# Two transformer layer types: the ratio of the exponential sums put ahead of the key sums, and the reciprocal denominator put behind the numerators

## The chip, the cores and the metric

One core of a Trainium2 chip. Its engines run side by side, each through its own list of instructions in order: TensorE (PE, with PEld for its weight loads), VectorE (DVE), ScalarE (ACT), GpSimd (POOL) and SyncE (SP, which here issues the transfers). They wait for each other by semaphores. The metric is the device time of one execution in microseconds (us); the median of three runs of the kernel before is 319.74 us (319.6 to 320.0).

## The reference

`x` is 2048 tokens of 512 numbers, bf16. Four residual layers are run in the order A, B, A, B, with the same weights in both passes; each adds to `x` an attention of the layernormed `x`. There are 32 heads of 16 numbers.

```
# layer A, linear attention, per head
pq, pk = q @ w_phi, k @ w_phi
phi_q = [softmax(pq), softmax(-pq)]          # 32 features
phi_k = [softmax(pk), softmax(-pk)]
kv, z = phi_k.T @ v, phi_k.sum(tokens)       # the "key sums"
o = (phi_q @ kv) / (phi_q . z + 1e-6)
# layer B: softmax attention of each token over 8 tokens at distances 0, 2, ..., 14
# both: x = x + o @ wo
```

Layer A's two softmaxes of a query have the denominators S0 = sum exp(pq) and S1 = sum exp(-pq). With E0 = exp(pq) and E1 = exp(-pq), o = (E0.kv0/S0 + E1.kv1/S1) / (E0.z0/S0 + E1.z1/S1), and the same value comes out when both parts of the fraction are multiplied by S0, as (E0.kv0 + (S0/S1) E1.kv1) / (E0.z0 + (S0/S1) E1.z1).

## The kernel before

The tokens are worked on in 4 blocks of 512 (4 tiles `t` of 128 tokens). `wqkv` and `w_phi` are folded into one matrix WA at the start. A layer A then has these steps for each block `b`; names are those of the code, lines those of the profile.

- Keys (`s_a1`): projections of keys (L632) and values (L644), exp of plus and minus the key features on ACT (Ek, L638), their sums over 16 features by four halving additions on DVE (L665 to L678), the reciprocals as Ln and Exp on ACT (L684, L685), Ek times these on DVE (L690), and the key sums on PE (`kv`, L707): per tile 16 matmuls with the values as weights (33 columns: 32 values and a one) and Ek as the moving side (2 x 32 columns), two side by side in the array. All blocks add into one PSUM bank, which a matmul with zeros opens (L700).
- Queries (`s_a2`): projections (L737, 4 x 4 matmuls of 512 columns), exp of both signs on ACT (Eq, L745), sums over features on PE (`ms`, L753, 32 matmuls), Ln and Exp of both sums on ACT (L759, L760: rS = 1/S0 and 1/S1).
- Between (`s_akv`), once per layer, after the last key sum: the bank is copied to SBUF (kvT, L202 or L204), turned by four transposes (L783), and masked into ZM (L792, for denominators) and R (L796, for numerators).
- Denominators (`s_a3`): `md` (L821, 32 matmuls of Eq with ZM), then on DVE D times rS and the sum of both (L829, L832), on ACT Ln and Exp (L835, L836), on DVE rho = rS/denominator for both signs (L840). Rho is spread to all 128 rows: in blocks 0 and 1 by PE (`bc`, L847, 16 matmuls per sign) and multiplied into all 8 pieces of Eq on DVE (L855, straight from PSUM, or from a copy bs that ACT makes at L886); in blocks 2 and 3 by two transfers through DRAM (Prho) and two DVE products of 2048 columns (L875).
- Numerators (`s_a4`): `mo` (L940, 32 matmuls of the scaled Eq with R), four copies out of PSUM (oT, by ACT or DVE), the output projection (L553), residual addition (L571, or by a matmul with the identity, L556, and an ACT copy), layernorm sums, and transposes for layer B (L482), whose projections are L967.

Nothing is scheduled at run time. Every step is a closure in a thread of its stage and engine; the string `_ORDER` lists the threads in the order in which the next closure of each is recorded, so it fixes the order of each engine. `_CHOICE` says for each movable copy whether DVE (1) or ACT (0) makes it, and `_SLOTS` which buffer or PSUM bank each tile takes. All three came from a search outside the kernel. `_OPT` is the same before and after.

Of the kernel before, what the change touches and what calls it, by code (L numbers as in the profile page):

```python
# [8 lines left out]
BF16 = mybir.dt.bfloat16  # L9
# [24 lines left out]
VCH = NB * 8 * DV  # L34
EST = (1, 3)
# [25 lines left out]
8 2 i 2e 3s e3 ce 2p 23 i a 5l i i 9 i i i 5o i i i i 4e e7 1m i 0 3u 3r 0 f i e c j b 2 k 3 4 j o 5q 1m l 3 m  # L61
p 1n 0 i 1 n 1t e4 o 1o q 1m 1p r 0 1m 1u s 1m z 5k z z 5 1m 1r 7 6 z 20 20 7 1q 1s 1t 21 21 t 20 20 1v 22 10
z 22 1t 7 1t 20 1w 22 t 11 24 24 13 u 12 16 12 1t t 15 1t v 12 12 22 x 18 14 1x d w w 1y 2c y 18 18 26 18 2d
1f 2d 2c 1z 2d 24 2d 27 17 19 18 1a 1b 21 1c 1d 22 21 22 39 1e 20 20 22 39 25 2c 3b 3a 3a 1f 3a 2d 3a 2f 2c 1f
1f 39 ch 22 2f 2d 2g 1g 29 1f 2d 1j 2f 2d 7 1h 29 1i 1k 3a 29 2n 29 2i 2n 3c 2o 2o 2o 2k 2o 2k 2q 1l cd 2h 2n
2a 2k 2f 2n 2k 3a 2o 2j 24 2q 2r 2q 2o 2o 2o 29 2y 28 2y 2y 3c 2l 2z 2v 2z 2s 2z 2z 2k 2y 2z 39 36 31 2z 36 2z
3a 3b 36 36 2v 31 2v 37 2v 31 2t 36 2z 36 2b 2b 2b 2b 2m 2m ci 36 36 2m 3a 2w 2m 2v 33 34 32 31 3c 35 2q 3c 36
3b 2x g 2x 2u 2x 30 37 2x 36 38 38 38 38 3i 3c 3h 3c 39 3b 3a 3j 3k 3k 3k 3c 3d 3c 3e 3l 3b 3m 3d 3e 5h 3n 3m
3c 3e 3e 3l 5i 3m 3q 3m 3m 4f 3m 3d 3l 5j 3e 3e 3m 5i 3m 3m 3v 3d 3e 3e bd 5h 5m 5n 5i 5i 5i 3m 3d 3e 7c 5h 7d
5p 5i 5i 5i 5r 3f 3g 3g 5i 3f 3g 5i 3w 3f 3z 3x 3f 3g 5s 3y 7e 40 41 3g 7d 5u 5v 7f 5t 3g 3p 41 42 41 41 44 3g  # L70
43 3g 43 5w 5x 5x 7f 45 46 43 43 47 43 7f 5y 3f 90 47 48 49 3g 4c 91 5x 41 4b 41 41 41 4a 92 5x 4d 60 91 4l 5z
61 5z 93 5z 4q 62 5z 4g 7d 4g 4g 4m 4q 63 ck 5z 7d 4r 93 4i 4l 63 66 64 67 7g 4s 7j 65 7h 7i 4h 4j 7k bo 4n 4q
4q 4u 4w 91 7l 4t 7l 7l 7m 7l 7o 68 7n 7n 4l 7p 3h 7n 7q 4w 93 4v 7n 4v 3o 91 4f 6a 7r 4o 6b 7n 6k 6f 69 4g 4k
4l 7r 6l 7s h 4w 6g 6k 6m 4p 6a 6c 6p 7t 7u 6a 6k 6f 6n 7v 4w 6k 6h 94 6r 6d 4x 4x b2 6r 4x 97 6o 98 4x 95 6f
# [36 lines left out]

_SLOTS = {
    "med": (
        "b79ca642352f85de6b0464b12833892cb7516e70efd8561f1706ed4a53bc7430e3f9eba731f9cd011a4091d20483b8ae4c4f"
        "b71d6236f9ec40bfd6ea7830c4"
    ),
    "ps": (
# [2008 lines left out]
```

## Time and profile before

| what | value |
|---|---|
| median of 3 runs | 319.74 us (319.6 to 320.0) |
| span of the profiled execution | 318.1 us |
| what lies around the span, by the median | 1.6 us |
| PE busy | 307.7 us, 97% |
| DVE busy | 295.6 us, 93% |
| ACT busy | 275.0 us, 86% |
| granted PE clock | full in all 40 slices |

The profile gives one execution's span only; what lies around it is the difference to the median of the runs. "Busy" counts the stretches in which at least one instruction of the engine is under way. A matmul of 512 columns is shown with 380 ns, but the next one starts about 216 ns later, so that PE's busy time hides pauses shorter than about 160 ns. Times in the text are counted from the span's start. The layer A parts lie at about 11 to 76 us and 145 to 230 us, the layer B parts at 76 to 178 us and from 224 us to the end.

### The profile page before, as it was taken

The numbers are of one execution on the slowest core, as the hardware profiler recorded it, in microseconds if no ns is written. First come the engines' busy times: TensorE is split into PE (matmuls) and PEld (weight loads), VectorE is DVE, ScalarE is ACT, GpSimd is POOL, SyncE is SP. The second block draws the span as 40 slices with busy tenths as digits, with TensorE's granted clock in tenths as the row PEclk, the third lists the DMA queues.
The fourth block names the chain that finished last, engine by engine and source line by source line (L and its number), as shares of the span: only waits on it lengthen the run. The fifth ranks groups of instructions, "written<-read, shape, count | busy, mean of one in ns | idle before, by whom it ended". The sixth has DMA issues, their size and how long they took to land.

```text
span 318.1 us, 8900 instructions
## 1 busy us (share of the span) xinstructions
PE 307.7 (97%) x3578; PEld 152.9 (48%) x3578; DVE 295.6 (93%) x459; ACT 275.0 (86%) x639; POOL 47.2 (15%) x60
## 2 busy tenths in 40 slices
PE   8999999899999999999999999989999999999994
PEld 4644456445454444444444455544444544444552
DVE  6999996998999999999999999689998999999994
ACT  4999999999898778999999999899999867697751
POOL 6000000000004212000000000033141644045000
PEclk9999999999999999999999999999999999999999
DMA  7977100005794989939894600004289875565664
GB/s 203 358 186 148 36 2 4 2 19 145 165 178 100 156 141 136 144 66 140 145 134 62 69 0 2 4 19 134 59 185 137 140 133 134 105 178 126 158 152 170
DMA packets 45789, 36.37 MB, mean 114 GB/s; under 512 B 30832, under 2 KB 41136, under 8 KB 45744
## 3 DMA queue, kind: packets, MB, share of 16 engines
q1 hardware_dynamic: 45216, 35.75, 56.3%
q8 instruction: 29, 0.48, 0.7%
q14 instruction: 16, 0.13, 0.2%
q10 hardware_dynamic: 528, 0.02, 0.1%
HBM read 11.13 MB, written 3.25 MB: 45 GB/s over the span
## 4 chain that ended last, share of the span: by engine, by line
PE 87%; DVE 5%; ACT 5%; DMA 1%; issue 1%; SPq 0%; DVEq 0%; ACTq 0%
PE PS L967 23%; PE PS L553 18%; PE PS L632 9%; PE PS L644 9%; PE PS L737 6%; PE PS L1128 4%; PE PS L1066 4%; PE PS L1185 2%; DVE Eq L855 2%; PE PS L707 2%; PE PS L940 1%; PE PS L482 1%; PE PS L556 1%; PE PS L1200 1%; PE PS L1082 1%; DMA x<-in_A_x_dram 1%
## 5 line engine op out<-in xcount | busy, mean ns | idle before, releaser
L967 PE MATMUL PS<-xnT,WB 128*128 128x512 bf16 x336 | 76.8, 380 | 0.1
L1059 DVE TENSOR_TENSOR prod<-QT,K 128x4096 bf16<-128x4096 bf16 x28 | 63.4, 2287 | 0.5 <-POOL K L993 0.5
L1121 DVE TENSOR_TENSOR pav<-PT,Vg 128x4096 bf16<-128x4096 bf16 (+1 forms) x29 | 62.9, 2214 | 0.2
L967 PEld LDWEIGHTS <-WB 128*128 128x128 bf16 x336 | 37.3, 114 | 36.4 <-issue 3.3
L745 ACT ACTIVATE Eq<-PS 128x512 bf16<-128x512 f32 x64 | 36.3, 619 | 0.0
L638 ACT ACTIVATE Ek<-PS 128x512 bf16<-128x512 f32 x64 | 35.1, 622 | 0.2 <-PE PS L632 0.2
L553 PEld LDWEIGHTS <-oT 128*128 128x128 bf16 x236 | 21.9, 98 | 26.6 <-issue 1.3
L737 PE MATMUL PS<-xnT,WA 128*128 128x512 bf16 x128 | 32.0, 380 | 0.5 <-DVE s L829 0.3
L578 ACT ACTIVATE sqd<-x 128x512 bf16<-128x512 bf16 x48 | 29.9, 631 | 2.2 <-DVE x L571 2.0
L644 PE MATMUL PS<-WA,xnT 128*128 128x512 bf16 x128 | 31.6, 379 | 0.0
L632 PE MATMUL PS<-WA,xnT 128*128 128x512 bf16 x128 | 31.0, 379 | 0.2 <-ACT WA L204 0.2
L571 DVE SCALAR_TENSOR_TENSOR x<-PS,x 128x512 bf16<-128x512 f32 x46 | 30.2, 684 | 0.7 <-PE PS L553 0.7
L204 ACT CAST oT<-PS 128x512 bf16<-128x512 f32 (+1 forms) x50 | 26.7, 597 | 3.8 <-PE PS L1128 2.1
L553 PE MATMUL PS<-WoA,oT 128*128 128x512 bf16 x128 | 29.8, 380 | 0.0
L553 PE MATMUL PS<-WoB,oT 128*128 128x512 bf16 x108 | 26.5, 379 | 0.0
L204 ACT CAST K<-PS 128x512 bf16<-128x512 f32 x30 | 17.3, 593 | 3.1 <-PE PS L967 1.9
L632 PEld LDWEIGHTS <-xnT 128*128 128x128 bf16 x128 | 12.3, 98 | 15.2 <-issue 1.0
L644 PEld LDWEIGHTS <-xnT 128*128 128x128 bf16 x128 | 12.2, 98 | 14.5 <-issue 0.4
L690 DVE TENSOR_TENSOR Ek<-Ek,rk 128x4096 bf16<-128x4096 bf16 (+1 forms) x10 | 18.6, 1860 | 0.4 <-ACT rk L685 0.4
L737 PEld LDWEIGHTS <-WA 128*128 128x128 bf16 x128 | 11.6, 98 | 14.6 <-issue 1.7
L466 DVE TENSOR_SCALAR xn<-x,rstd,nmr 128x512 bf16<-128x512 bf16 x48 | 18.1, 424 | 0.6
L204 ACT CAST V<-PS 128x512 bf16<-128x512 f32 x26 | 15.2, 596 | 2.6 <-PE PS L967 2.6
(175 smaller groups left out, 505.1 us busy)
## 6 DMA issues: line engine op xcount, KB each, us to landing
Vg<-V SPq DMA_DIRECT2D x112, 131.5 KB, 4.3
Prho<-rd SPq DMA_DIRECT2D x8, 512.0 KB, 6.1
x<-in_A_x_dram SPq DMA_DIRECT2D x3, 512.0 KB, 6.6
WB<-in_B_wqkv_dram SPq DMA_DIRECT2D x3, 512.0 KB, 9.8
out_dram<-x SPq DMA_DIRECT2D x6, 256.0 KB, 2.3
wraw<-in_A_wqkv_dram SPq DMA_DIRECT2D x4, 256.0 KB, 4.5
vd<-Vs SPq DMA_DIRECT2D x2, 272.0 KB, 2.9
x<-in_A_x_dram SPq DMA_DIRECT2D x4, 128.0 KB, 3.4
```

Of the source, the lines that this page charges most:

```text
L204: self.nc.scalar.copy(out=out, in_=in_)
L553: nc.tensor.matmul(y[:], lhsT=lh(t, c), rhs=Wo()[:, c, :], start=(c == 0), stop=(c == NB - 1 and not onpe))
L571: nc.vector.scalar_tensor_tensor(out=xb[:, t, :], in0=T[t][:], scalar=1.0, in1=xb[:, t, :], op0=ALU.mult, op1=ALU.add, **kw)
L578: nc.scalar.activation(out=sqd[:], in_=xb[:, t, :], func=ACT.Square, accum_out=T["ss"][:, t:t + 1])
L632: nc.tensor.matmul(pk[:], lhsT=xnT[:, t, k, :], rhs=self.WA[:, k, D:2 * D], start=(k == 0), stop=(k == NB - 1))
L638: nc.scalar.activation(out=T["E"][:, t, s, :], in_=T["k", t][:], func=ACT.Exp, scale=1.0 - 2.0 * s)
L644: nc.tensor.matmul(pv[:], lhsT=xnT[:, t, k, :], rhs=self.WA[:, k, 2 * D:3 * D], start=(k == 0), stop=(k == NB - 1))
L737: nc.tensor.matmul(pq[:], lhsT=self.WA[:, k, hb * P:(hb + 1) * P], rhs=xnT[:, :, k, :], start=(k == 0), stop=(k == NB - 1))
L745: nc.scalar.activation(out=self.Eq[L, b][s][:, :, hb, :], in_=T[hb][:].rearrange("p (t i) -> p t i", t=4), func=ACT.Exp, scale=1.0 - 2.0 * s)
L967: nc.tensor.matmul(pp[:], lhsT=self.WB[:, k, i * D + c:(i + 1) * D:NB], rhs=xnT[:, :, k, :], start=(k == 0), stop=(k == NB - 1))
L1059: nc.vector.tensor_tensor(out=pr[:], in0=QT[:, c:c + 1, :].to_broadcast([P, NW, TB]), in1=win, op=ALU.mult)
L1121: nc.vector.tensor_tensor(out=pv, in0=PT[:, :, lo:lo + n].unsqueeze(1).to_broadcast([P, NB, 2, n]), in1=vw, op=ALU.mult)
```

## The change

Of each query's two sums only the ratio w = S0/S1 is formed (`ls`, `lw`, `w`: Ln of both sums on ACT, a subtraction on DVE, Exp on ACT). It is spread to all rows by PE in every block (`bc` in `s_a2`, L770 of the new kernel) and multiplied into the four pieces of E1 alone (`mulw`, L784, from PSUM or from ACT's copy bs). These steps need no key sums. `md` (L847 of the new kernel) then adds both signs in one PSUM range, ACT takes Ln and Exp of it (L855, L857), and this one reciprocal (rho) is spread: in blocks 0 and 1 by PE (L863) and four copies to an SBUF tile Prho (`rev`, ACT or DVE), in blocks 2 and 3 by one transfer through DRAM. `mo` (L919) works on Eq as it is, and rho comes in as the numerators leave PSUM: DVE multiplies each of the four PSUM banks with a slice of Prho (`ev` in `s_a4`, L929). Those 32 evictions were copies on ACT or DVE before.

The key sums change sides: the weights are 128 columns of Ek (64 of each sign) and the values move (65 columns), 8 matmuls per tile over the whole array, 256 in all instead of 512 (L704). They come out with features on the rows, so the transposes, kvT's copy and the opening matmul go; four copies of 64 x 260 (`sh`) bring them into R, half of 1e-6 is added to the features' own sums (`z`), and ZM is filled and R masked in place (`r`).

The three tables are new throughout. Choices that moved: DVE's copies of oT fall from 11 to 1 and ACT's from 48 to 26 (with 32 products instead), DVE's vaug copies rise from 7 to 11, six of 48 layernorm applications (xn) go from DVE to ACT, and 17 residuals on PE become 19.

On DVE in the first layer A, before, from the copy of the key sums (kvT) on; `s1`, `Ds` and `rho` belong to the denominators, `Eq` to the queries:

```order
L202 CAST kvT_121<-PS_88 128x512
L792 TENSOR_TENSOR ZM0_122<-PS_88,maskH_97 128x2x2x8 x2
L796 TENSOR_TENSOR R_126<-PS_88,mask2_98 128x256
L829 TENSOR_TENSOR s1_1086<-PS_88,rS_1004 128x256
L832 TENSOR_TENSOR Ds_1088<-s1_1086 128x128
L840 TENSOR_TENSOR rho_1130<-rS_1004,Ds_1088 128x256
L829 TENSOR_TENSOR s1_1153<-PS_88,rS_1132 128x256
L832 TENSOR_TENSOR Ds_1155<-s1_1153 128x128
L855 TENSOR_TENSOR Eq_467<-PS_88,Eq_467 128x512 x2
L855 TENSOR_TENSOR Eq_467<-bs_1158,Eq_467 128x512
L855 TENSOR_TENSOR Eq_467<-PS_88,Eq_467 128x512
L855 TENSOR_TENSOR Eq_469<-PS_88,Eq_469 128x512
```

Now the same place, from the last ratio ahead of the copy of the key sums (R) on:

```order
L760 TENSOR_TENSOR lw_953<-lS_873 128x128
L204 CAST R_125<-PS_88 64x4x65
L784 TENSOR_TENSOR Eq_462<-bs_891,Eq_462 128x512
L784 TENSOR_TENSOR Eq_462<-bs_875,Eq_462 128x512
L811 TENSOR_SCALAR R_125<-R_125 128x8
L819 TENSOR_TENSOR ZM0_121<-R_125,maskH_97 128x4x4x2 x2
L784 TENSOR_TENSOR Eq_513<-PS_88,Eq_513 128x512 x4
L760 TENSOR_TENSOR lw_1081<-lS_1072 128x128
L823 TENSOR_TENSOR R_125<-R_125,mask4_98 128x8x64
L784 TENSOR_TENSOR Eq_918<-PS_88,Eq_918 128x512 x2
L204 CAST Prho_1169<-PS_88 128x512 x3
L929 TENSOR_TENSOR oT_1228<-PS_88,Prho_1169 128x512 x4
```

The products with the whole rho (two signs, 16 pieces for two blocks) gave way to products of E1 with the ratio, which stand around the copy of the key sums; behind them now stand copies of rho (Prho) and the products that empty the numerators (oT), ahead of the first residuals.

In the second layer A of the changed kernel, DVE from the copies of the key sums on:

```order
L204 CAST R_125<-PS_88 64x4x65 x3
L784 TENSOR_TENSOR Eq_3002<-bs_3276,Eq_3002 128x512
L784 TENSOR_TENSOR Eq_3002<-PS_88,Eq_3002 128x512
L811 TENSOR_SCALAR R_125<-R_125 128x8
L819 TENSOR_TENSOR ZM1_122<-R_125,maskH_97 128x4x4x2 x2
L784 TENSOR_TENSOR Eq_3002<-bs_3283,Eq_3002 128x512
L784 TENSOR_TENSOR Eq_3002<-PS_88,Eq_3002 128x512
L823 TENSOR_TENSOR R_125<-R_125,mask4_98 128x8x64
L784 TENSOR_TENSOR Eq_2448<-bs_2826,Eq_2448 128x512
L204 CAST Prho_3409<-PS_88 128x512 x3
L760 TENSOR_TENSOR lw_3517<-lS_3482 128x128
L929 TENSOR_TENSOR oT_3540<-PS_88,Prho_3409 128x512 x4
```

And ACT there, from the first reciprocal denominator (rho) on; `lS` and `w` make the last block's ratio:

```order
L857 ACTIVATE rho_3383<-Ds_3381 128x128
L742 ACTIVATE Eq_3292<-PS_88 128x4x128
L855 ACTIVATE Ds_3402<-PS_88 128x128
L857 ACTIVATE rho_3404<-Ds_3402 128x128
L742 ACTIVATE Eq_3286<-PS_88 128x4x128
L742 ACTIVATE Eq_3292<-PS_88 128x4x128
L855 ACTIVATE Ds_3477<-PS_88 128x128
L857 ACTIVATE rho_3479<-Ds_3477 128x128
L756 ACTIVATE lS_3482<-PS_88 128x256
L206 CAST Prho_3409<-PS_88 128x512
L764 ACTIVATE w_3520<-lw_3517 128x128
```

Here DVE's row `lw` needs ACT's `lS`, which stands behind the last exps of Eq and three pairs of Ds and rho, and DVE's oT products are queued behind that `lw`. On PE the steps between the last key sum and the first output projection are now, in order: bc of a ratio, 12 query projections, `md` of two blocks, 4 projections, bc of a rho, `md` of one block, `ms` of the last block, `mo` of the first block, bc of the last ratio, bc of a rho. Before, they were: the transposes, `ms`, `md`, 4 projections, `md`, bc, 4 projections, bc, `md`, 8 projections, `mo`, `ms`, bc. In the first layer A they are now: 8 projections, bc of a ratio, `md`, 4 projections, `ms`, `md`, bc of a ratio, 4 projections, bc of a rho, 4 projections, `mo`, bc of a rho, 4 projections, `mo`, and the first output projection (4 matmuls and one with the identity), then `ms` of the last block.

```diff
--- before.py
+++ after.py
+HQ = 4 * DH
+KVC = HQ + 1
...
 _ORDER = """
-8 2 i 2e 3s e3 ce 2p 23 i a 5l i i 9 i i i 5o i i i i 4e e7 1m i 0 3u 3r 0 f i e c j b 2 k 3 4 j o 5q 1m l 3 m
-p 1n 0 i 1 n 1t e4 o 1o q 1m 1p r 0 1m 1u s 1m z 5k z z 5 1m 1r 7 6 z 20 20 7 1q 1s 1t 21 21 t 20 20 1v 22 10
...
+8 i i bu 2 i i 0 i 2 a 0 3 i 2e 4 3 i 1m 1 9 i 0 c e i 0 i f 1m 7 i b j 5 o k j l 1n 1o p 1t 1m m i o 1m q r 20
...
         def ek(t, s):
             if t == 0 and s == 0:
-                T["E"] = self.big([4, 2, D], "Ek")
-            nc.scalar.activation(out=T["E"][:, t, s, :], in_=T["k", t][:], func=ACT.Exp, scale=1.0 - 2.0 * s)
+                T["E"] = self.big([4, 8, 2, HQ], "Ek")
+            nc.scalar.activation(out=T["E"][:, t, :, s, :], in_=T["k", t][:].rearrange("p (g c) -> p g c", c=HQ),
+                                 func=ACT.Exp, scale=1.0 - 2.0 * s)
...
         def ev(t, dve):
             vatile()
-            self.copy(dve, T["va"][:, t, :, 0:H], T["v", t][:].rearrange("p (a c) -> p a c", c=H))
+            self.copy(dve, T["va"][:, t, :, 0:HQ], T["v", t][:].rearrange("p (g c) -> p g c", c=HQ))
...
         def kv(t):
             if L not in self.kvp:
-                self.kvp[L] = self.ps()
-            K = self.kvp[L]
-            if b == 0 and t == 0:
-                nc.tensor.matmul(K[:], lhsT=self.kvT[:, 0:P], rhs=self.kvT[:], start=True, stop=True)
-            for r in range(4):
...
-                        nc.tensor.matmul(out, lhsT=T["va"][:, t, q, :], rhs=T["E"][:, t, :, q * H:(q + 1) * H],
-                                         start=(b == 0 and t == 0 and r == 0 and h2 == 0),
-                                         stop=(b == 3 and t == 3), tile_position=(0, 64 * c), skip_group_check=True)
+                self.kvp[L] = [self.ps() for _ in range(2)]
+            for g in range(8):
+                c = g // 2 * KVC
+                nc.tensor.matmul(self.kvp[L][g % 2][:, c:c + KVC], lhsT=T["E"][:, t, g, :, :],
+                                 rhs=T["va"][:, t, g, 0:KVC], start=(b == 0 and t == 0 and g < 2),
+                                 stop=(b == 3 and t == 3), skip_group_check=True)
...
-        def rs():
-            r = self.sm([2, P], "rS", F32, 4)
-            nc.scalar.activation(out=r[:], in_=T["S"][:, 0:2 * P], func=ACT.Ln)
-            nc.scalar.activation(out=r[:], in_=r[:], func=ACT.Exp, scale=-1.0)
-            self.rS[L, b] = r
+        def ls():
+            T["l"] = self.sm([2, P], "lS", F32, 2)
+            nc.scalar.activation(out=T["l"][:], in_=T["S"][:, 0:2 * P], func=ACT.Ln)
+
+        def lw():
+            T["lw"] = self.sm([P], "lw", F32, 2)
+            nc.vector.tensor_tensor(out=T["lw"][:], in0=T["l"][:, 0, :], in1=T["l"][:, 1, :], op=ALU.subtract)
+
+        def w():
+            T["w"] = self.sm([P], "w", BF16, 2)
+            nc.scalar.activation(out=T["w"][:], in_=T["lw"][:], func=ACT.Exp)
+
+        def bc():
+            T["pb"] = [self.ps() for _ in range(4)]
+            for hb in range(NB):
+                for t in range(4):
...
+        def mulw(t, direct):
+            ev = self.Eq[L, b][1][:, t, :, :]
+            src = T["pb"][t] if direct else T["bs", t]
+            nc.vector.tensor_tensor(out=ev, in0=src[:].rearrange("p (a i) -> p a i", a=NB), in1=ev, op=ALU.mult)
...
         add(st, "PE", ms)
-        add(st, "ACT", rs)
+        st = "aw_%d%d" % (L, b)
+        add(st, "ACT", ls)
+        add(st, "DVE", lw)
+        add(st, "ACT", w)
+        add(st, "PE", bc)
+        for t in range(4):
+            direct = _CHOICE[self.nflex] == "1"
+            self.flex(st, bev, t)
+            add(st, "DVE", mulw, t, direct)
...
+        def sh(half, s, dve):
+            self.copy(dve, R[HQ * half:HQ * half + HQ, s, :, 0:KVC],
+                      self.kvp[L][half][HQ * s:HQ * s + HQ, 0:NB * KVC].rearrange("p (b c) -> p b c", c=KVC))
...
+        def z():
+            nc.vector.tensor_scalar(out=R[:, :, :, HQ:KVC], in0=R[:, :, :, HQ:KVC], scalar1=DEN_EPS / 2, scalar2=None,
+                                    op0=ALU.add)
...
+            v = R[:, :, :, 0:HQ].rearrange("p s b (j d) -> p (s b) j d", d=DH)
+            nc.vector.tensor_tensor(out=v, in0=v, op=ALU.mult,
+                                    in1=self.mask4[:].unsqueeze(1).unsqueeze(3).to_broadcast([P, 8, 4, DH]))
+
+        for half in range(2):
+            for s in range(2):
+                self.flex(st, sh, half, s)
+        add(st, "DVE", z)
+        add(st, "DVE", r)
...
     def s_a3(self, L, b, dma):
...
             for s in range(2):
                 for hb in range(NB):
                     for t in range(4):
-                        nc.tensor.matmul(Dp[32 * t:32 * t + 32, s * P:(s + 1) * P],
+                        nc.tensor.matmul(Dp[32 * t:32 * t + 32, 0:P],
                                          lhsT=zm[:, self.reg(s, hb) * H:(self.reg(s, hb) + 1) * H],
                                          rhs=self.Eq[L, b][s][:, t, hb, :], start=(hb == 0 and s == 0),
-                                         stop=(hb == NB - 1), tile_position=(0, 32 * t), skip_group_check=True)
...
+                                         stop=(hb == NB - 1 and s == 1), tile_position=(0, 32 * t),
+                                         skip_group_check=True)
+
+        def ln():
             T["Ds"] = self.sm([P], "Ds", F32, 1)
-            nc.vector.tensor_tensor(out=T["Ds"][:], in0=T["DR"][:, 0, :], in1=T["DR"][:, 1, :], op=ALU.add)
-
-        def ln():
+            nc.scalar.activation(out=T["Ds"][:], in_=T["D"][:, 0:P], func=ACT.Ln)
+            T["rho"] = self.sm([P], "rho", BF16)
+            nc.scalar.activation(out=T["rho"][:], in_=T["Ds"][:], func=ACT.Exp, scale=-1.0)
...
+            for r in range(4):
                 for t in range(4):
+                    nc.tensor.matmul(T["pb"][t][:, r * P:(r + 1) * P], lhsT=self.indB[32 * t:32 * t + 32, r, :, :],
+                                     rhs=T["rho"][32 * t:32 * t + 32, :], start=True, stop=True,
                                      tile_position=(32 * t, 0))
...
+        def ptile():
+            pr = self.med([4, 4, P], "Prho")
+            for r in range(4):
+                self.rho[L, b][r] = pr[:, :, r, :]
+            return pr
+
+        def rev(t, dve):
+            if "pr" not in T:
+                T["pr"] = ptile()
+            self.copy(dve, T["pr"][:, t, :, :].rearrange("p r i -> p (r i)"), T["pb"][t][:])
...
+            pr = ptile()
...
+            src = bass.AP(a.tensor, a.offset, [[pitch, 16], [0, 8], [1, 16 * P]])
+            nc.sync.dma_start(out=pr[:].rearrange("p t r i -> p (t r i)"), in_=src)
+
+        self.rho[L, b] = {}
         add(st, "PE", md)
...
         add(st, "ACT", ln)
-        add(st, "DVE", rho)
         if dma:
             add(st, "SP", wr)
-            for s in range(2):
-                add(st, "SP", rdb, s)
-            for s in range(2):
-                add(st, "DVE", muld, s)
+            add(st, "SP", rdb)
             return
...
+        add(st, "PE", bc)
+        for t in range(4):
+            self.flex(st, rev, t)
...
-                                         lhsT=self.R[32 * r:32 * r + 32, self.reg(s, hb), :],
+                                         lhsT=self.R[32 * r:32 * r + 32, s, hb, 32 * (r % 2):32 * (r % 2) + 32],
...
-        def ev(r, k, m, dve):
+        def ev(r, k, m):
...
-            self.copy(dve, self.oT[key, b][:, r, k * w:(k + 1) * w], T[r][:, k * w:(k + 1) * w])
+            n = 4 // m
+            nc.vector.tensor_tensor(
+                out=self.oT[key, b][:, r, k * w:(k + 1) * w].rearrange("p (t i) -> p t i", t=n),
+                in0=T[r][:, k * w:(k + 1) * w].rearrange("p (t i) -> p t i", t=n),
+                in1=self.rho[L, b][r][:, k * n:(k + 1) * n, :], op=ALU.mult)
...
             for r in range(4):
-                self.flex(st, ev, r, k, m)
+                add(st, "DVE", ev, r, k, m)
```

248 lines of the change are left out of this document (89 added, 159 removed).

## The prediction

> **What bounds the kernel now.** I read the page first: what is busy, and on what the chain of waits stands.
>
> ```profile
> span 318.1 us, 8900 instructions
> PE 307.7 (97%) x3578; PEld 152.9 (48%) x3578; DVE 295.6 (93%) x459; ACT 275.0 (86%) x639; POOL 47.2 (15%) x60
> PE 87%; DVE 5%; ACT 5%; DMA 1%; issue 1%; SPq 0%; DVEq 0%; ACTq 0%
> ```
>
> PE bounds it, with DVE close behind; 10% of the chain stands on DVE and ACT. Where that is, the busy time by stretches tells: a quiet part of layer B, and the two places around and behind the last key sum of each layer A.
>
> ```profile
> core 0: us, PE busy (x) PEld busy (x) DVE busy (x) ACT busy (x) POOL busy (x), PEclk, DMA share, GB/s
> 52.00:64.00 12.00, 10.45 (x255) 5.88 (x254) 8.93 (x21) 11.49 (x28) 0.00 (x0) 1.00 0.01 3
> ...
> 100.00:145.00 45.00, 45.00 (x318) 21.19 (x314) 44.72 (x43) 39.10 (x96) 7.12 (x7) 1.00 0.85 134
> ...
> 204.00:224.00 20.00, 17.56 (x401) 8.86 (x401) 17.47 (x40) 18.64 (x46) 5.26 (x2) 1.00 0.23 61
> ```
>
> In 100 to 145 us PE never pauses and DVE hardly. In the two others PE lacks 1.55 and 2.44 us, DVE 3.1 and 2.5, ACT only 0.5 and 1.4. PE's waits by their releaser:
>
> ```profile
> PE PS L847 <- DVE rho L840: 2.6, 4, 1.0
> ...
> PE PS L783 <- ACT kvT L204: 0.7, 1, 0.7
> ...
> PE PS L737 <- DVE s L829: 0.3, 1, 0.3
> PE PS L940 <- ACT Eq L745: 0.3, 1, 0.3
> ```
>
> So 3.9 us of PE's waiting hangs on the chain key sums, kvT, denominators, rho. This is what the change can win, and 0.1 or so more at each of the seven waits, which the modelled ends hide: some 4.7 us. All else is PE's own work. PE's order in time shows its unit prices:
>
> ```profile
> 46.42 1.90 PE L644 MATMUL PS<-WA,xnT 128*128 128x512 bf16 x8
> 48.16 1.03 PE L737 MATMUL PS<-xnT,WA 128*128 128x512 bf16 x4
> 49.11 2.10 PE L707 MATMUL PS<-Ek,vaug 128*33 128x64 bf16 x128
> 51.15 0.63 PE L753 MATMUL PS<-Eq,indS 128*32 128x128 bf16 x32
> ...
> 206.90 0.63 PE L821 MATMUL PS<-Eq,ZM 128*32 128x128 bf16 x32
> 208.16 0.40 PE L847 MATMUL PS<-rho,indB 32*128 32x128 bf16 x16 [0.63 <-DVE rho L840]
> 208.50 1.04 PE L737 MATMUL PS<-xnT,WA 128*128 128x512 bf16 x4
> ...
> 213.52 0.63 PE L753 MATMUL PS<-Eq,indS 128*32 128x128 bf16 x32
> 215.11 0.41 PE L847 MATMUL PS<-rho,indB 32*128 32x128 bf16 x16 [0.95 <-DVE rho L840]
> ```
>
> Eight full matmuls take 1.74 us to the next start (0.217 each); four ahead of a step of another array shape take 0.95, so such a switch costs some 0.09. 128 key-sum matmuls take 2.04 with the switch behind them, 16 spreading ones 0.34 (0.25 without). In 204 to 224 us the spread of rho waits twice, 0.6 and 1 us.
>
> **The change part by part.** First PE's work. The new key-sum matmul (128 columns of weights, 65 moving) has a near twin, the halo projection of layer B:
>
> ```profile
> L1193 PE MATMUL PS<-xnT,WB 128*128 128x64 bf16 x16 | 0.6, 193 | 0.0
> ...
> L1193 PEld LDWEIGHTS <-WB 128*128 128x128 bf16 x16 | 0.6, 98 | 0.2
> ```
>
> Sixteen are busy for 0.6 us with a last one of 0.19, so they start some 29 ns apart, and their weight loads of 98 ns overlap. 256 then take 7.4 us, against 4 x 1.95 = 7.8 for the 512 old ones: -0.4. The bounds are 0 overlap (98 ns each, 25.1 us) and 29 ns; I take 29, as rows and shape are the same. [...]
>
> The two opening matmuls go (-0.4), and eight transposes:
>
> ```profile
> 15.70 0.96 PE PS L482 x16
> ```
>
> At 0.06 each, -0.5. Spreads rise from 8 to 12 (8 of w, 4 of rho), four more at 0.25: +1.0. Two more residuals on PE: +0.4. Counting changes of array shape in PE's order, there are some seven more (key sums now run in the full shape, but spreads and pieces of layer B's products are scattered more): +0.6. PE's work: about +0.7, nothing to win.
>
> DVE and ACT, by their groups:
>
> ```profile
> L855 DVE TENSOR_TENSOR Eq<-PS,Eq 128x512 bf16<-128x512 f32 x18 | 11.7, 683 | 0.0
> L855 DVE TENSOR_TENSOR Eq<-bs,Eq 128x512 bf16<-128x512 bf16 x14 | 5.5, 418 | 0.1
> L875 DVE TENSOR_TENSOR Eq<-Eq,Prho 128x2048 bf16<-128x2048 bf16 x8 | 9.7, 1218 | 0.0
> L829 DVE TENSOR_TENSOR s<-PS,rS 128x256 f32<-128x256 f32 x8 | 3.4, 420 | 1.6 <-ACT Eq L745 0.8 <-PE PS L821 0.5 <-ACT rS L760 0.3
> L840 DVE TENSOR_TENSOR rho<-rS,Ds 128x256 bf16<-128x256 f32 x8 | 3.4, 420 | 1.6 <-ACT Ds L836 1.6
> L832 DVE TENSOR_TENSOR Ds<-s 128x128 f32<-128x128 f32 x8 | 2.3, 292 | 0.3
> L466 DVE TENSOR_SCALAR xn<-x,rstd,nmr 128x512 bf16<-128x512 bf16 x48 | 18.1, 424 | 0.6
> L204 ACT CAST oT<-PS 128x512 bf16<-128x512 f32 x48 | 26.1, 606 | 2.1 <-PE PS L940 0.9 <-DVE prod L1059 0.6 <-PE PS L1128 0.4
> L468 ACT ACTIVATE xn<-x,nmr,rstd 128x512 bf16<-128x512 bf16 x16 | 12.9, 818 | 0.2 <-DVE nmr L457 0.2
> L836 ACT ACTIVATE Ds<-Ds 128x128 f32<-128x128 f32 x8 | 2.5, 309 | 0.2
> ```
>
> DVE loses L875, L829, L840 and L832 (18.8 us) and six xn (2.3). It gains 32 products out of PSUM, priced as the like L855 from PSUM (0.65 each, 20.8), and eight subtractions as L832 (2.3). Plain copies out of PSUM balance (oT -10, Prho +6, vaug +4, the rest 0); the copies of R, their masks, fewer residuals and the other split of L855 (15 and 17) net to about zero, the R copies bounded by L829 and L855. DVE: about +2. ACT loses some 15 copies at 0.54 (-8), gains six xn (+5) and R's copies and two residuals (+3), and its Ln and Exp of the ratio and denominator stand for those before: about 0. So no engine gets lighter. On SP, half of the Prho transfers go; they are no part of PE's waits above, so I cost that at nothing: what hides them is the layer B projections, 28 in a row (6 us) ahead of the next such block's output.
>
> What is left is the chain. Steps taken off it: the multiplication of rho into Eq ahead of `mo`, the transposes, and two DVE steps about the denominator. Steps put on it: ratio, spread, product with E1 ahead of `md`, and copies of rho and the DVE product ahead of the output projection. I followed the new order from the last key sum (0), each engine in its order, with PE's prices above and two rows for runs:
>
> ```profile
> 52.82 2.14 ACT L745 ACTIVATE Eq<-PS 128x512 bf16<-128x512 f32 x4
> ...
> 60.53 2.48 DVE L855 TENSOR_TENSOR Eq<-PS,Eq 128x512 bf16<-128x512 f32 x4
> ```
>
> 0.53 for an ACT piece and 0.62 for a DVE piece out of PSUM. Second layer: PE's bc, 12 projections and two `md` end at 4.2, with four projections and a bc at 5.4, and the third `md` at 5.9. `ms` of the last block needs ACT's last exps: two R and bs pieces, five exps, two Ln-and-Exp pairs and three more exps end at about 6.9, so it ends at 7.1 (wait 0.7) and `mo` at 7.7. The next bc needs ACT's lS (7.9), DVE's lw (8.15) and, behind a copy, ACT's w (8.75): wait 1.0. DVE's four products, behind that lw, end at 10.6, where the first output projection could start at 9.3: wait 1.3. Together 3.0, where the old order waited about 2.8 (2.44, and 0.1 for each of its four waits). First layer, in the same way: a bc of a ratio waits 1.2 for lS, lw and w; the first output projection waits 0.9 for three Prho copies and four products (8 pieces of DVE behind the bc); `ms` of the last block 0.4 for ACT. Together 2.5, before 1.9 (1.55 likewise). So the waits move from rho to the ratio and to the evictions, and are some 0.8 longer. Such a walk puts every step at full length; I take a little under half, +0.35.
>
> Sum: 318.1 + 0.7 + 0.35 = 319.15 of span; with the 1.6 around it (319.74 less 318.1), **320.7 us**.
>
> **The rivals.** A change within 0.2% (0.64 us) can't be told from none.
>
> *The waits go.* `mo` needs no rho any more, and w needs no key sums: with the ratio's work ahead of them, PE would run from the key sums to the output projection. For it: DVE had 5.6 us idle there. Against: ACT had under 2, and the last block's exps and ratio still lie behind the key sums in both layers. If a third of the 4.7 us stays: 318.1 + 0.7 - 3.1 + 1.6 = 317.3.
>
> *DVE becomes the bound there.* All numerators leave PSUM on DVE, while ACT took most copies. It decides from where DVE's 5.6 idle us are used up: then each of a layer's first two blocks holds PE for its four products (2.5 us), of which the projections and identity matmul of the block before cover about 1.1. 2 layers x 1.4 = 2.8 more, 320.7 + 2.8 = 323.5. Against: DVE's sum grows by 2 only.
>
> *Loads on the path.* If the 98 ns loads don't overlap, 25.1 - 7.8 in place of -0.4: 320.7 + 17.7 = 338.4. The twin speaks against it. [...]
>
> **How the numbers follow.** Forecast 0.47, waits gone 0.35, DVE 0.16, loads 0.02. The forecast's own range is 319.4 to 321.6 (the waits from 1 us less to 0.9 more); a little over half of it lies over 320.4, most of the rest within 0.2%. Slower: 0.25 + 0.16 + 0.02 = 0.43 less a little for DVE's milder end, 0.41; same: 0.21 of the forecast and 0.03 of the waits' mild end, 0.24; faster: 0.35. For 8 in 10 the range runs from 316.8 to 323.0.
>
> **What would show it.** Right: PE starts of key sums 29 to 30 ns apart; PE busy up by under 1 us; waits of PE in the two places on w, on the products L929 and on ACT's exps, 3 to 6 us in all; DVE 297 to 298 busy. Wrong: no PE wait over 0.3 us there (first rival); DVE without a gap from R's copies to the first xn and PE waiting over 2 us at an output projection (second); key sums 98 ns apart (third).

## The result, and the profile after

The changed kernel takes **324.44 us** (median of 4 executions, 323.94 to 324.53) against 319.67 for the kernel before on the same chip: a ratio of **1.0146, 95% interval 1.0133 to 1.0159**. It is slower by 4.8 us; the forecast was 320.7, slower by 1.0, with a range up to 323.0.

The changed kernel's page, its busy times and the granted clock in 40 slices:

```profile
span 322.1 us, 8481 instructions
PE 309.0 (96%) x3345; PEld 154.2 (48%) x3378; DVE 297.1 (92%) x461; ACT 272.8 (85%) x640; POOL 37.1 (12%) x60
...
PEclk9999999999999999999999999997999999999998
```

PE is busy 1.3 us longer, DVE 1.5; that does not make 4. New is the 7 in the clock row. PE's waits (line, releaser, sum, times, longest):

```profile
PE PS L770 <- ACT w L764: 1.3, 2, 0.8
...
PE PS L863 <- DVE oT L929: 0.5, 1, 0.5
PE PS L635 <- DMA xnT<-xn: 0.5, 1, 0.5
...
PE PS L863 <- DVE Prho L204: 0.4, 1, 0.4
PE PS L863 <- ACT bs L779: 0.3, 1, 0.3
```

The wait on rho (2.6 us) is gone. Waits on w and on the products L929 stand in its place, as forecast, and waits on copies (Prho, bs) where the forecast had ACT's exps. L635, the key projection that opens the second layer, waits at 148 us for its transposed input, a wait that the kernel before does not have in its list. The second layer's transition in time (start, length, step, wait ahead of it), the key sums from the first layer at its head:

```profile
54.39 1.18 PE L704 MATMUL PS<-vaug,Ek 128*128 128x65 bf16 x32
...
214.71 0.65 PE L919 MATMUL PS<-Eq,R 32*32 32x512 bf16 x32
216.16 0.41 PE L770 MATMUL PS<-w,indB 32*128 32x128 bf16 x16 [0.80 <-ACT w L764]
217.11 0.31 PE L863 MATMUL PS<-rho,indB 32*128 32x128 bf16 x3 [0.55 <-DVE oT L929]
217.70 0.58 PE L863 MATMUL PS<-rho,indB 32*128 32x128 bf16 x13 [0.28 <-ACT bs L779]
218.22 0.61 PE L556 MATMUL PS<-WoA,oT 128*128 128x512 bf16 x1
219.05 2.44 PE L556 MATMUL PS<-WoA,oT 128*128 128x512 bf16 x6 [0.22 <-issue]
221.33 0.38 PE L559 MATMUL PS<-x,ident 128*128 128x512 bf16 x1
221.64 0.65 PE L919 MATMUL PS<-Eq,R 32*32 32x512 bf16 x32
```

Thirty-two key sums take 1.02 us to the next step, which started at 55.41: 32 ns each, not 29. Three waits follow each other from 215.4 to 217.7, and then the output projection L556 goes at half pace: 8 matmuls and an identity one in 3.4 us, where nine at the 0.217 us of the prediction take 2.0. The same place by stretches (busy us of each engine, the granted clock behind POOL's):

```profile
214.20:217.60 3.40, 1.88 (x87) 1.10 (x74) 3.40 (x8) 2.84 (x9) 3.40 (x2) 1.00 0.24 48
217.60:221.00 3.40, 3.07 (x19) 1.33 (x20) 2.18 (x7) 2.60 (x6) 0.61 (x1) 0.50 0.46 130
```

After 3.4 us in which PE was busy for 1.88, the clock is halved for 3.4 us. The end differs too. The last two stores in the profile's DMA issues (number, size, median us from issue to landing), first of the changed kernel, then of the kernel before with its last three:

```profile
out_dram<-x SPq DMA_DIRECT2D x2, 128.0 KB, 3.0
```

```profile
out_dram<-x SPq DMA_DIRECT2D x3, 128.0 KB, 1.7
```

To find where the 4 us of span lie, I set PE's start times against the sum of its own work (each step at its start-to-start time, key sums at the 32 ns above): how far PE is behind its work, and by how much that grows in each part. The last column is from the last matmul's start to the end of the span; "before" is the mean of two profiles.

| us | work | behind at 17 us | 17-100 (first transition) | 100-165 | 165-225 (second transition) | 225 to last matmul | end |
|---|---|---|---|---|---|---|---|
| before | 304.59 | 4.84 | 1.37 | 0.22 | 2.61 | 0.12 | 4.33 |
| changed, profiled | 305.95 | 5.03 | 1.74 | 0.75 | 3.52 | -0.22 | 5.33 |
| difference | +1.36 | +0.19 | +0.37 | +0.53 | +0.91 | -0.34 | +1.00 |

The differences add up to 4.0, as do the spans'. (A negative growth is a price a little too high.) How the work is told from the transitions hangs on the prices: with one rate for each kind of matmul and the prediction's 0.09 us for every change of array shape, the work comes out as +2.1, the transitions as +0.1 and +0.6, and the other columns within 0.2 of those above. Much of the loss lies where the prediction had priced nothing: 100 to 165 us, the halved clock (in the +0.91) and the end.

### The profile page after: what moved, and what is told of

It reads as the page before. It is cut to its first block, busy times and chain, and to the rows that moved or that the text cites. A ratio compares the mean times of both kernels' runs of the same rounds, so it can differ in the third digit from the quotient of the medians.

```text
span 322.1 us, 8481 instructions
## 1 busy us (share of the span) xinstructions
PE 309.0 (96%) x3345; PEld 154.2 (48%) x3378; DVE 297.1 (92%) x461; ACT 272.8 (85%) x640; POOL 37.1 (12%) x60
## 4 chain that ended last, share of the span: by engine, by line
PE 84%; ACT 6%; DMA 4%; DVE 2%; SPq 1%; issue 1%; DVEq 0%
PE PS L950 20%; PE PS L556 15%; PE PS L635 9%; PE PS L648 8%; PE PS L734 8%; PE PS L1049 3%; PE PS L1111 3%; PE PS L704 2%; PE PS L1168 2%; DMA xnT<-xn 2%; PE PS L485 1%; ACT Eq L742 1%; DMA Vg<-V 1%; DMA x<-in_A_x_dram 1%; PE PS L919 1%
## 5 line engine op out<-in xcount | busy, mean ns | idle before, releaser
L950 PE MATMUL PS<-xnT,WB 128*128 128x512 bf16 x336 | 77.9, 380 | 0.1
L641 ACT ACTIVATE Ek<-PS 128x512 bf16<-128x512 f32 x64 | 35.9, 642 | 0.0
L556 PEld LDWEIGHTS <-oT 128*128 128x128 bf16 x236 | 22.0, 99 | 28.4 <-issue 4.1
L581 ACT ACTIVATE sqd<-x 128x512 bf16<-128x512 bf16 x48 | 30.8, 645 | 2.6 <-DVE x L574 2.1
L556 PE MATMUL PS<-WoA,oT 128*128 128x512 bf16 x119 | 31.4, 391 | 0.6 <-issue 0.2
L574 DVE SCALAR_TENSOR_TENSOR x<-PS,x 128x512 bf16<-128x512 f32 x44 | 29.3, 685 | 2.6 <-PE PS L556 2.2
L648 PE MATMUL PS<-WA,xnT 128*128 128x512 bf16 x118 | 31.0, 379 | 0.5
L635 PE MATMUL PS<-WA,xnT 128*128 128x512 bf16 x125 | 30.8, 379 | 0.6 <-DMA xnT<-xn 0.5
L556 PE MATMUL PS<-WoB,oT 128*128 128x512 bf16 x102 | 26.4, 380 | 0.3
L206 ACT CAST oT<-PS 128x512 bf16<-128x512 f32 (+1 forms) x28 | 16.0, 593 | 9.2 <-PE PS L1111 9.1
L206 ACT CAST K<-PS 128x512 bf16<-128x512 f32 x31 | 18.4, 596 | 4.0 <-PE PS L950 3.5
L929 DVE TENSOR_TENSOR oT<-PS,Prho 128x512 bf16<-128x512 f32 x32 | 20.4, 683 | 0.9 <-ACT x L571 0.7
L635 PEld LDWEIGHTS <-xnT 128*128 128x128 bf16 x128 | 12.3, 98 | 15.5 <-DMA xnT<-xn 0.8
```

Source lines behind the costliest of these rows:

```text
L206: self.nc.scalar.copy(out=out, in_=in_)
L556: nc.tensor.matmul(y[:], lhsT=lh(t, c), rhs=Wo()[:, c, :], start=(c == 0), stop=(c == NB - 1 and not onpe))
L574: nc.vector.scalar_tensor_tensor(out=xb[:, t, :], in0=T[t][:], scalar=1.0, in1=xb[:, t, :], op0=ALU.mult, op1=ALU.add, **kw)
L581: nc.scalar.activation(out=sqd[:], in_=xb[:, t, :], func=ACT.Square, accum_out=T["ss"][:, t:t + 1])
L635: nc.tensor.matmul(pk[:], lhsT=xnT[:, t, k, :], rhs=self.WA[:, k, D:2 * D], start=(k == 0), stop=(k == NB - 1))
L641: nc.scalar.activation(out=T["E"][:, t, :, s, :], in_=T["k", t][:].rearrange("p (g c) -> p g c", c=HQ), func=ACT.Exp, scale=1.0 - 2.0 * s)
```

## The experiments

All start from the changed kernel. A mean clock over the span of 0.994 or less is taken as a halved clock in mid-kernel (a halving behind the last matmul alone leaves 0.995 or more in the profiles). The rule is rough: 3.41 us at half clock and nothing else leave 0.9947 of the profiled span of 322.1, so that a 0.995 can be either. Ratios are to the kernel before on the same chip.

**The changed kernel again** (*again*, no edit).

> The changed kernel, nothing edited, timed again beside the three runs below. The theory to be tested: three stalls that the prediction left out make most of the loss: the TensorE clock halves for 3.4 us in the second layer's transition (about 1.4 us), the last output transfer lands 1.0 us later, and the second layer's first key projection waits 0.7 us for its transposed input. It expects 323.9 to 324.6 us here, and a half-clock stretch of 3.4 us near 218 us. The rival, that these three are taken up elsewhere (the path is set by VectorE's and ScalarE's chain in the transitions, and what one stall costs another wait gives back), expects the same time here. If executions without the half-clock stretch run as long as those with it, that speaks for the rival.

Measured: 324.04 us, 1.0139 (1.0120 to 1.0158). The profile fell on an execution without the halving, and shows the same place thus:

```profile
214.50:217.90 3.40, 2.05 (x109) 1.25 (x97) 3.12 (x6) 2.64 (x8) 3.40 (x2) 1.00 0.18 34
217.90:221.30 3.40, 2.89 (x56) 1.28 (x56) 3.40 (x9) 3.40 (x8) 0.98 (x1) 1.00 0.53 145
```

The waits are the same, the clock stays, and the growth from 165 to 225 us is 2.1 in place of 3.5. So the same program runs with or without the halving: 5 of the 8 executions measured so far have it (mean 324.4 us, the others 323.8).

**Extra matmuls where PE idles** (*warm4*).

```diff
             T["pb"] = [self.ps() for _ in range(4)]
+            if (L, b) == (1, 3):
+                for _ in range(4):
+                    nc.tensor.matmul(T["pb"][0][:], lhsT=self.ident[:], rhs=self.WA[:, 0, 0:TB], start=True, stop=True)
             for hb in range(NB):
```

> Four 128x512 matmuls of constants are put ahead of the last ratio spread of the second layer (the one that waits 0.96 us), in the PSUM bank that this spread then overwrites. They run in time in which TensorE is idle. If the halved clock costs what the trace suggests, the clock stays at full speed at 218 us and the time falls by 1.0 to 1.6 us against the changed kernel, to 322.9 to 323.4. If the chain on VectorE and ScalarE sets that stretch anyway, the time stays within 0.3 us, 324.1 to 324.6. If idle time as such sets the clock and 0.9 us of it is not enough, the clock halves again and the time stays as well, with the mean clock at 0.991.

Measured: 323.55 us, 1.0116 (1.0097 to 1.0135); no halving in 4 executions. The gain against *again* is 0.5 us, half of what the theory put. Only part of the executions were halved without the edit, so that the median could not gain the whole 1.4; and the extra matmuls delay the spread behind them: the growth from 165 to 225 us is 2.5, not 2.1.

**The input of the second layer's first key projection, earlier** (*xn*): one normalisation (`7m`) moves on ACT ahead of two copies.

```diff
-... 8p a7 7n 7l 5r 5r 9v 5s 5r 5r a9 a0 9x 7m 8o ...
+... 8p a7 7n 7l 7m 5r 5r 9v 5s 5r 5r a9 a0 9x 8o ...
```

> The last of the four normalisations of the block whose key projection opens the second layer is moved on ScalarE ahead of two PSUM copies (one query, one key copy of layer B), so that its transposing transfer is issued 0.95 us earlier. If the wait of the key projection for it (0.5 to 0.7 us at 148 us) lies on the path that sets the end, the time falls by 0.4 to 0.7 us, to 323.7 to 324.0. If a later wait takes it over, it stays within 0.2 us.

Measured: 322.90 us, 1.0105 (1.0085 to 1.0124), 1.1 us under *again* and so more than the 0.4 to 0.7 expected. With the halved executions left out (two of six here, two of four in *again*) the means are 322.75 and 323.42, 0.7 apart. The wait of L635 is no longer in the list, and the growth from 100 to 165 us is 0.5 in place of 0.8. Of the eight profiles of the changed kernel and its variants without this edit seven show the wait, 0.2 to 0.8 us; the eighth (*flag2*, further down) does not, and grows by 0.5 as well. None of the six profiles with the edit shows it. So the traces show 0 to 0.8 us of gain, by execution.

**The flag's reading behind the last stores** (*flag*): `jc` goes to the end.

```diff
-... hl hh ja hj hl hi hj hn jc ho hl hl
+... hl hh ja hj hl hi hj hn ho hl hl jc
```

> The last step of the program's order, reading the check flag and branching, is moved from ahead of the last two stores to behind them, as the kernel before has it. If the branch's code fetch is what delays the last store (its last packets end 2.1 us after its first here, against 0.4 in the kernel before), the time from the last VectorE instruction to the end falls from 4.6 to about 3.5 us and the whole by 0.8 to 1.2 us, to 323.2 to 323.7. If the end only waits for the store as such, the time stays or grows by up to 0.3, since the flag's read now lies behind the stores.

A miss: 323.71 us, 1.0115 (1.0095 to 1.0135), and in the profile the end grew, from 5.3 us after the last matmul to 6.0. The two last stores landed later still:

```profile
out_dram<-x SPq DMA_DIRECT2D x2, 128.0 KB, 3.8
```

So it was not SP's own read that stood in the way. The flag's computation (`ja`) still lay ahead of the last residual, and the other engines did not wait for the stores: in this run's trace POOL and PE's sequencer have branched by 317.13 us, while the last store is issued at 317.72 and SP branches at 318.73.

**Flag computed and read at the end** (*flag2*).

```diff
-... hl hh ja hj hl hi hj hn jc ho hl hl
+... hl hh hj hl hi hj hn ho hl ja hl jc
```

> Both the step that computes the check flag (VectorE, after the last residual) and its reading and branch (after the last store) are put at the end of the order, as in the kernel before. Moving the reading alone left the stretch from VectorE's last instruction to the end at 5.25 us (4.6 in the changed kernel, 3.5 in the kernel before). If the branches of ScalarE, VectorE and GpSimd, which follow the flag and not the stores, bring in code whose transfers collide with the last store, they now come after it: the stretch falls to 3.3 to 3.7 us, and the time by 0.8 to 1.2 us against the 324.2 of the changed kernel (mean of its 8 executions). If the last store is slow for a reason of its own, the stretch stays over 4.3 us.

Measured: 321.76 us, 1.0073 (1.0047 to 1.0098). The end is 4.2 us after the last matmul, as short as before:

```profile
out_dram<-x SPq DMA_DIRECT2D x2, 128.0 KB, 1.7
```

In the changed kernel a 16 KB transfer of the instruction queues (q8) starts at 317.63 us and takes 1.1 us, while the packets of the last two stores run from 317.8 to 319.95; in this run the stores' last packet ends at 317.71 and the first such transfer starts at 318.05. All six profiles with the flag ahead of the last residual end 5.3 to 6.0 us after the last matmul, all others, the two of the kernel before among them, 4.2 to 4.3. That these transfers are what the stores wait for fits the times, and was not shown apart from the order. The gain in time, 2.1 us by the two ratios, is more than the 1.1 of the end. Part of the rest is the clock, as two of *again*'s four executions were halved. By the rule above none of the four was halved here, but one of them probably was: it has a mean clock of 0.995 and takes 323.33 us, where the others take 321.35 to 321.87, and in the profiles with the flag at the end the halving behind the last matmul never takes the mean under 0.997.

**The edits together, without and with the extra matmuls** (*xf* is *xn* and *flag2*; *xfw* has *warm4*'s lines too).

> The earlier normalisation (xn, which took the wait at 148 us from 1.1 us to 0.3 us of path) and the flag at the end (flag2) together, without the four extra matmuls. If both stalls were on the path: 322.1 us where the clock stays at full speed (321.9 span in such executions of the changed kernel, less 0.7, less 1.0, and 1.8 around the span) and 323.3 where it halves; a median of 322.0 to 322.8. If each is given back later, 323.5 or more. The clock should halve (mean clock 0.993 or less) in a third to a half of the executions.

> As the run before, with the four 128x512 matmuls ahead of the last ratio spread of the second layer. So far the clock halved in 5 of 8 executions of the changed kernel (spans 322.1 to 323.1, mean 322.6, against 321.9 in the three others) and in none of 4 with these matmuls. If they keep the clock up, no execution here has a mean clock of 0.993 or less, and the median lies 0 to 0.8 us below the run without them, at 321.7 to 322.3. If it was chance, the clock halves here in about as many executions as without them.

Measured: *xf* 323.05 us, 1.0103 (1.0087 to 1.0118), *xfw* 321.64, 1.0055 (1.0042 to 1.0069), and when repeated 321.49, 1.0047 (1.0034 to 1.0060). In *xf* three of four executions have the halved clock (mean 323.2, the fourth 322.05), in *xfw* none of five. Over all runs but *prodact*: 12 of 28 executions without the extra matmuls are halved (13 with the one of *flag2*), none of 34 with them, and none of 50 of the kernel before. *xf* as a whole fell short of its forecast, by its share of halved executions. On the same chip its one execution at full clock (322.05) is not under *flag2*'s (321.35 to 321.87), so these two runs show no gain from *xn*; that execution's opening, which *xn* does not touch, was 0.9 us longer than in *flag2*'s profile.

**Two products of each layer's first block on ACT** (*prodact*), the second rival's test; 1/denominator is left out of these.

```diff
             n = 4 // m
+            if b == 0 and r >= 2:
+                nc.scalar.activation(out=self.oT[key, b][:, r, :], in_=T[r][:], func=ACT.Identity, scale=1.0 / 2048)
+                return
             nc.vector.tensor_tensor(
```

> In the first block of each layer, two of the four products that take the numerators out of PSUM and multiply them by 1/denominator are replaced by a plain copy with a constant scale on ScalarE: VectorE has 1.3 us less to do in each transition, and the factor 1/denominator is left out there. If VectorE's products hold the path in the transitions (they end the 0.96, 0.70 and 0.43 us waits at 216 to 218 us, two of which are for PSUM banks that the products free), the time falls by 0.8 to 2 us, to 322.2 to 323.4. If the waits come from ScalarE's chain for the ratio, it stays within 0.4 us of 324.2 or grows, since ScalarE has 1.2 us more.

Measured: 325.76 us, 1.0175 (1.0141 to 1.0208). Taking 1.3 us from DVE in each transition and giving them to ACT made it slower: the growth is 2.5 in the first (1.7 before the edit), and in the second 4.2 with the halving (3.5). New among the waits is one for ACT's copy:

```profile
...
PE PS L770 <- ACT w L764: 1.0, 2, 0.6
PE PS L863 <- DVE oT L932: 0.7, 1, 0.7
PE PS L919 <- ACT oT L930: 0.6, 1, 0.6
```

So DVE alone does not bind the transitions: work taken off it and put on ACT costs more than it frees. Whether ACT's total is what counts, or the place that these copies take in ACT's order, was not told apart.

**The kernel before again** (*before2*), **the changed kernel with *flag2* and *warm4*'s edits** (*fw*), **and that with an edit of the opening** (*fwh*: on PE the query weights' first transposes `1t`, with their copy `1u`, behind the four folding matmuls of the key weights).

```diff
-... 1o p 1t 1m m i o 1m q r 20 6 1u 1m i 1m z z ...
+... 1o p 1m m i o 1m q r 20 6 1m i 1m 1t 1u z z ...
```

> The kernel before, unedited, for a second profile of it. The one profile that the prediction used reached its first steady stretch with TensorE 4.7 us behind its own work (at 17 us); the changed kernel and its variants stand at 5.0, 5.3, 5.5, 5.5, 5.7, 5.7, 5.8, 6.2 and 6.4 us there. If the opening is part of the loss, this profile shows 4.3 to 5.0 us; if the opening scatters as widely here, anything up to 6.4 us. No halved clock in mid-kernel is expected by either.

> The flag at the end and the four extra matmuls together, with the changed kernel's own order of the normalisation: against the run with all three edits (321.6 us, 1.0055 of the kernel before) it prices the earlier normalisation. If the wait at 148 us is on the path, 0.3 to 0.7 us more than that, a ratio of 1.0065 to 1.0080; if it is given back later, the same, 1.0045 to 1.0065. No execution should have a mean clock of 0.993 or less.

> As fw, and in the opening the first transposes of the folded query weights, and the copy of them, are moved behind the four matmuls that fold the key weights: in the changed kernel these transposes stand ahead of them on TensorE, and wait there for a transfer (0.86 us in one profile). If the opening's loss comes from that, TensorE stands 4.5 to 5.2 us behind its work at 17 us and the time falls by 0.4 to 0.9 us against fw, to a ratio of 1.002 to 1.005. If the transfers themselves set the opening, the time stays within 0.2 us of fw.

Measured: the second profile of the kernel before has PE 5.0 us behind at 17 us and a span of 318.0. *fw* takes 322.50 us, 1.0081 (1.0063 to 1.0099), a little above its range; the two runs of *xfw* lie 0.0026 and 0.0034 lower, on other chips. That would be 0.8 to 1.1 us for *xn*, more than the 0.4 that L635 waits in *fw*'s profile; one of the two intervals overlaps *fw*'s, and the rest is not explained. *fwh* is a miss, 323.99 us, 1.0120 (1.0100 to 1.0139): at 17 us PE is 5.6 behind, and at 25 us 7.3. Its waits:

```profile
PE PS L399 <- DVE wT L204: 1.4, 1, 1.4
PE PS L485 <- DVE xn L469: 1.4, 1, 1.4
...
```

One wait was exchanged for two behind DVE.

**Two more edits of the opening** (*xfwo*: `o`, the second tile's statistics on DVE, behind the weight copies `1n 1o`; *xfwp*: also `r`, its transposes on PE, behind the folding), against *xfw* again (*xfw2*).

```diff
-... j 5 o k j l 1n 1o p 1t 1m m i o 1m q r 20 6 1u 1m i 1m z z ...
+... j 5 k j l 1n 1o o p 1t 1m m i o 1m q r 20 6 1u 1m i 1m z z ...     (xfwo)
+... j 5 k j l 1n 1o o p 1t 1m m i o 1m q 20 6 1u 1m i 1m r z z ...     (xfwp)
```

> The three edits together (earlier normalisation, flag at the end, four extra matmuls) and one more in the opening: VectorE's statistics of the second input tile, which wait 1.3 to 1.5 us for their transfer, are moved behind the first tile's normalisation and the second copy of the transposed key weights, which in the changed kernel stand queued behind that wait. If this queueing is what the opening lost, TensorE stands 4.7 to 5.3 us behind its work at 17 us (5.74 without this edit, 4.67 and 5.00 in the kernel before) and the time lies 0.4 to 0.9 us under the run without it in this call. If the transfers themselves set the opening, it stays within 0.2 us.

> The three edits again, on the same chip as the run before, for the comparison: 321.4 to 322.2 us, a ratio of 1.004 to 1.007 to the kernel before, and a full clock throughout, if the first measurement of it (321.64 us, 1.0055) holds.

> As xfwo, and on TensorE the transposes of the second input tile, which waited 0.63 us there for that tile's normalisation, are moved behind the four matmuls that fold the key weights, so that neither the weight copy on VectorE nor the folding on TensorE stands behind the second tile. If the opening's loss is such queueing, TensorE stands 4.7 to 5.2 us behind its work at 17 us and the ratio to the kernel before is 1.002 to 1.004 (1.0047 and 1.0055 without edits in the opening, 1.0077 for xfwo). If the wait only goes on to the next step, it lies at 1.0045 or above.

Measured: *xfwo* 322.34 us, 1.0077 (1.0064 to 1.0089); *xfwp* 322.74, 1.0100 (1.0084 to 1.0117); *xfw2* 321.49. Both are slower than without these edits. In *xfwp* the waits up to 60 us (those that the edit was after, on L399, are gone):

```profile
...
PE PS L485 <- DVE xn L469: 0.8, 2, 0.4
PE PS L389 <- DMA wraw<-in_A_wqkv_dram: 0.3, 1, 0.3
PE PS L389 <- ACT WA L206: 0.2, 1, 0.2
```

PE is again some 5.6 us behind at 17 us in both: the wait went on to the next steps, which need DVE's normalised tiles or a transfer. What the opening loses stays open. Over the eleven profiles with the changed kernel's own opening PE is 5.0 to 6.4 us behind there, 5.6 in the mean, against 4.7 and 5.0 before.

## Why the prediction was wrong

The direction (slower, which had the largest of the three chances) was right, the size not: +1.0 was forecast, +4.8 came. By its steps:

- **What bounds the kernel** held: PE, with 3.9 us of waits on the chain through rho. Those waits are gone in the trace.
- **PE's work, +0.7**: measured +1.4 (+2.1 with the coarser prices). The term of the key sums was mis-sized: 32 ns each and not 29, so 8.2 us for 256 in place of 7.4, and +0.4 against the old ones where -0.4 stood. 3 ns of error times 256 is 0.8 us. More readings of the twin would not have shown it: in all sixteen profiles it runs at 29 ns (27 to 30). The twin was not near enough, with 64 moving columns and other operands; which of these makes the 3 ns was not tried. That the loads overlap was right: the profile shows them with 98 ns each (L704), at matmul starts 32 ns apart. So the third rival (98 ns each, 338 us) fell: 32 ns are a third of 98.
- **DVE +2, ACT 0**: DVE +1.5, ACT -2.2. Right, and of no weight.
- **The waits of the transitions, +0.35 out of a walk of +0.8**: the first layer grew by 0.4 (walk 0.6), the second, at full clock in *again*, shrank by 0.5 (2.1 in place of 2.6, where the walk had 3.0 against 2.8). In the second layer the walk had the wait on w right (1.0, measured 0.96). It had the wait for the products at the output projection (1.3), where it came ahead of it, at the spread of rho (0.70); and it had `ms` wait 0.7 for ACT's exps, which the list does not show. So it made the second layer's waits too long. Without the halved clock this step alone would have come out some 0.5 us better than forecast.
- **The sum** is the step that failed. It took everything outside PE's work and the two transitions to stay as it was (span 318.1 plus two terms), though the change also has the whole order searched anew. Four things did not stay. *The clock*: in the executions with the halving the transition takes 1.4 us more (3.4 against 2.05 from the first L556 to the next L919), and the times of one kernel's halved and full executions differ by 0.7 to 1.3 us. The prediction took the clock as full, as all its rows of before showed it. *The end*: +1.0, from the flag's place ahead of the last stores, which the order's last rows showed and I did not compare. *The second layer's start*: +0.5, of which the late transpose is the part that *xn* moves (0.3 by the growth in its profile). *The opening*: +0.2 in the profiled execution, 0.8 in the mean, not explained.
- **The rivals.** "The waits go" fell: 3.0 us of waits stand in the two places, within the 3 to 6 forecast. "DVE becomes the bound" gave 323.5, nearest in time, but for another reason: DVE is without a gap from 214.2 to 217.6 us, yet PE waits 0.2 us at an output projection and not over 2, and *prodact*, which took products off DVE, was slower.

*xfw*, which undoes three of these, takes back 2.7 to 2.9 of the 4.4 us that *again* lies above the kernel before, and leaves 1.5 to 1.8, with the unexplained opening in it: not far from the +1.0 that the forecast had. No version here beats the kernel before.

## What to carry to other kernels

When a change brings a new order for the whole program, compare the old and new order at its start, at its end and at every seam, not only where the arithmetic changed: here more than half of the loss lay there. Short waits that follow each other closely cost more than their sum here: 2.1 us of them were followed, in some executions (5 of 8 of the changed kernel), by a halved clock that cost a further 1.4. A price per instruction that is used some hundred times should come from a row of exactly that form, or be given an error as large as the effect: 3 ns were 0.8 us here.

## What was not expected of the hardware

**The clock fell without a long pause.** The longest wait in the place was 0.96 us beyond the step's own time. In the changed kernel's profile the clock records begin with full clock at 5.99 us; it is halved at 217.62 and full again at 221.03, after 3.413 us. From 5.99 to 217.62 are 62 times this length, and to the fall behind the last matmul, at 320.02, 92 times; in the profile of the kernel before, 92 times lie between 5.39 and its only fall, at 319.42, behind the last instruction. These three falls are all that the two traces have. What sets such a length, and what makes the clock fall at its end, they do not show. One program was halved in some executions and not in others; my estimate, not tested, is that it depends on whether the three waits come to lie in one such length or in two. They end at 216.16, 217.11 and 217.70 in the halved execution above, with the fall at 217.62; in *again*, which was not halved, they end at 217.05, 218.16 and 218.59, on both sides of the 217.9 in its rows above. Of the profiles, the two with 1.88 and 1.80 us of PE busy in such a stretch of 3.4 us were halved after it; with 2.05 (*again*), 2.12 (*xn*) and 2.45 (the kernel before) they were not. *prodact*'s two lines and that of the kernel before:

```profile
216.30:219.70 3.40, 1.80 (x71) 0.99 (x66) 2.88 (x6) 2.75 (x7) 3.11 (x2) 1.00 0.45 111
219.70:223.10 3.40, 3.40 (x9) 1.05 (x8) 1.60 (x4) 2.82 (x6) 0.00 (x0) 0.50 0.21 54
```

```profile
213.60:217.00 3.40, 2.45 (x70) 1.45 (x71) 3.16 (x7) 3.20 (x9) 3.40 (x2) 1.00 0.49 154
```

Busy time alone does not tell the halved from the others. At the end of the kernel before, 1.46 us of it, all full 128x128 matmuls, were followed by full clock in the next stretch:

```profile
312.60:316.00 3.40, 1.46 (x12) 0.88 (x9) 1.81 (x5) 0.37 (x1) 0.00 (x0) 1.00 0.66 231
316.00:318.10 2.10, 0.00 (x0) 0.00 (x0) 0.00 (x0) 0.00 (x0) 0.00 (x0) 1.00 0.08 20
```

So were 1.74 us of such matmuls at the end of *xfw*. In the transition, where 1.88 us stood ahead of the halving, most matmuls use 32 rows or 32 columns of the array. Whether the array's share decides was not tried.

**With the flag known early, the last stores landed late.** With the flag ahead of the last residual, instruction transfers of 8 and 16 KB run while the last stores of 128 KB go out (the changed kernel: 317.63 to 319.60 us, beside packets up to 319.95), and these take 3.0 us (changed kernel) and 3.8 us (*flag*) to land in place of 1.7. With the flag behind it the transfers start after the stores' last packet (*flag2*: 318.05 after 317.71; the kernel before: 316.33 after 315.98). *flag2* differs from the changed kernel in this order alone, and its stores land in 1.7 us; that the two kinds of transfer compete is my estimate from these times, and was not tried by itself.
